# A hand-ordered attention and mixture kernel: the order of all engines and the PSUM banks from row 2 on, drawn anew

## The chip, the cores and the metric

The kernel runs on one core of a Trainium2 chip. The metric is the device time of one execution in microseconds (us). The core has five engines that run side by side, each with its own instruction queue that is worked off in order: TensorE (PE, matrix products; its weight loads are shown as PEld), VectorE (DVE), ScalarE (ACT), GpSimd (POOL) and SyncE (SP, which here only issues transfers). Sixteen DMA engines move data between device memory (HBM) and the on-chip memory (SBUF). Matrix products land in PSUM, which has eight banks. Engines wait for each other by semaphores.

## The reference

Eight batch rows, eight heads, 576 tokens, head size 64. Half of the heads see the last 32 tokens, the other half every fourth of the last 128:

```python
    scores = scale * np.matmul(q, k.transpose(0, 1, 3, 2))
    mask_plain = (rel >= 0) & (rel < window)
    mask_dil = (rel >= 0) & (rel < window * dilation) & (rel % dilation == 0)
    scores = np.where(masks[None, :, :, :], scores, -1000000000.0)
    attn = np.exp(scores - max); attn = attn / sum
    x = np.matmul(attn, v)
```

What the heads of a token give, side by side, is a vector x of 512. A gate picks two of eight experts, and each adds a product of rank 16:

```python
    logits = x @ w_gate
    topk = the two largest; w = softmax of their logits
    out = x + sum over the two experts of w * ((x @ A[e]) @ B[e])
```

## The kernel before

The kernel is a list of small steps and a text, PLAN, that says in which order they are issued. The engine of a step is fixed, and so each engine gets the steps of the text that are its own, in the text's order. "S041@4" means that step S041 takes PSUM banks from number 4 on. A step waits for the steps that make its inputs, for those that last read a buffer that it overwrites, and, where it is the first user of its banks, for all users that these banks had before. The waits are worked out from the text when the program is built. So a new text changes two things: what stands ahead of a step in its engine's queue, and whose banks it has to wait for.

A step's name has a letter, sometimes a part, then the batch row r (0 to 7) and the group of heads g (0 plain, 1 dilated). S041 is the first part of the scores of row 4, group 1. For one row the work runs like this:

| step | engine | line | what it does |
|---|---|---|---|
| L, Lk, Lq, Lv | POOL issues | 272, 275 | loads of the row's q, k and v into one of four buffers, changed to bf16 on the way; L4 to L6 are two transfers each; row 7 comes in eight pieces (Lq7gh, Lv7gh) |
| S0rg, S1rg | PE | 212 | scores of five and of four blocks: 24 and 20 matmuls, two banks |
| E0rg, E1rg | ACT | 345 | exponential of these scores |
| Vrg | PE | 212 | 26 matmuls with v, three banks |
| Rrg, Nrg | DVE | 381, 384 | reciprocal of the sums, and the division |
| Brg | POOL | 391 | cast to bf16 (half of B71 is Bx7, on ACT) |
| Trg, Ur | PE | 408, 432 | transposes, 8 and 2 matmuls |
| Crg, Cdr, Cpr | ACT | 418 to 442 | copies of these to SBUF (Cx7 on DVE) |
| Z0r, Z1r | PE | 212 | products with A and the gate, 12 and 8 matmuls |
| Y0r, Y1r | ACT | 466 | copies to SBUF |
| m0, m1, s12, tt, top, g2 | DVE | 478 to 488 | gate values: the two largest logits, and their weights; th (ACT, 485) is a step in the middle of it |
| gzr | POOL | 493 | weights times the products (row 7: DVE) |
| Gr | PE | 498 | transposes, 5 matmuls (row 7: G7, H7) |
| gnr, gcr | ACT | 517, 514 | copies of these |
| Dr0, Dr1, Dr2 | PE | 212 | products with B, 4 matmuls each |
| Ar0, Ar1, Ar2 | DVE | 545, 575 | added to x; for late rows parts go by way of ACT (dx 571, dy 551) to POOL (A42 to A72 573; A53, A63, A73 553) |
| Or | SP | 586, 590 | store of the row; two halves for rows 6 and 7 |

F0 to F3 and "warm" are matmuls on zeros whose results nobody reads; pz, vz and xz set parts of buffers to zero, and cc and cd build the mask constants.

Line 212 is the helper that issues nearly all matmuls, so most TensorE rows of the profile carry it, and the names of the tiles tell them apart: "ps<-one" and "ps<-con,one" open a score step (24 or 20 matmuls, of which the first four write the mask), "ps<-in" are the rest of it, "ps<-in,p" is V, "ps<-aw,xt" is Z, "ps<-bt,gn" and "ps<-bt,gc" are D.

Rows overlap: while row r's scores are made, the adapters (T to A) of the rows before it are still on their way. A load of row r may start when row r-4 has used its buffer for the last time. All transfers of a queue run in the order in which they are issued. The stores wait for the last pieces of row 7's load (all Lq, and Lv710 and Lv711), and store number n also for the landing of store number n-2:

```python
            if name[0] == "O":
                if len(name) == 2:
                    o.deps = o.deps + stores[-2:-1]
                stores.append(name)
```

The order that the banks set is made here:

```python
            if o.bank is not None and o.bank.users[0] == name:
                o.bank.at = int(at)
                for b in range(o.bank.at, o.bank.at + o.bank.size):
                    o.deps = o.deps + held[b]
                    held[b] = list(o.bank.users)
```

Of the kernel before, what the change touches and what calls it, by code (L numbers as in the profile page):

```python
# [593 lines left out]


PLAN = """
pz0 wz warm@4 F1@1 awf btf vz00 pz2 con vz10 Lk00 Lk01 Lv00 Lv01
S000@6 vz01 vz11 tab cc1 cd3 vz20 cc0 vz21 cd2 cd0 L11 pz1 E000
F2@1 L10 cd1 S100@4 S101@6 E100 E101 L2 S001@2 E001 V00@4 R00 N00 V01@1
L3 R01 F0@0 xz0 B00 N01 B01 T00@4 vz30 L4 pz3 C00 S111@5 E111  # L600
awc S011@2 U0@0 T01@7 E011 V11@3 Cd0 Cp0 S010@1 C01 R11 vz31 E010 N11
Z00@0 Y00 m00 Z10@6 Y10 m10 S110@4 B11 s120 E110 tt0 th0 top0 V10@2
g20 gz0 T11@5 R10 N10 btc G0@1 gc0 D01@6 B10 gn0 D00@0 C11 xz1
U1@4 Cd1 Cp1 T10@5 C10 A01 A00 S121@6 E121 S120@3 S021@1 Z01@0 E021 Z11@5
Y01 m01 Y11 m11 L5 s121 S020@1 D02@0 V21@5 E120 top1 tt1 th1 g21
E020 A02 V20@0 R21 N21 R20 gz1 G1@5 gn1 F3@6 S130@6 N20 gc1 B21 E130
S031@3 D12@2 E031 S030@0 D10@5 T21@7 E030 C21 A12 S131@3 B20 V30@0 A10 E131
U2@7 T20@6 R30 N30 Cp2 B30 L6 V31@3 Cd2 C20 Z02@7 Y02 Z12@1 R31
N31 B31 T30@2 D11@6 Y12 C30 S041@4 A11 E041 S141@2 S140@6 m02 E141 S040@0
m12 s122 tt2 U3@5 Cp3 th2 E040 top2 Cd3 g22 gz2 V41@2 T31@0 E140  # L610
C31 V40@5 R41 N41 Z03@2 G2@0 Y03 gn2 Z13@1 gc2 R40 Y13 N40 B40
S051@2 D20@4 E051 A20 m13 S151@6 E151 Lq700 S050@0 S150@2 E150 m03 s123 V51@5
top3 tt3 T40@3 th3 Lq701 E050 C40 B41 g23 T41@4 C41 R51 Lq710 V50@0
N51 R50 D22@5 N50 U4@7 gz3 Cd4 Cp4 G3@6 gn3 D21@3 gc3 A22 A21
Z04@7 Y04 B50 Lq711 S060@0 D32@2 Z14@7 S161@5 m04 E060 Y14 m14 E161 s124
S160@0 A32 Lv710 T50@7 E160 D30@3 S061@5 top4 V60@0 A30 tt4 R60 C50 Lv711
O1 E061 B51 T51@3 N60 C51 V61@4 th4 g24 R61 N61 U5@7 S171@2 Cp5
Cd5 S070@0 Z05@7 E171 E070 Z15@6 Y05 S170@2 S071@4 Y15 Lv700 m05 m15 top5
Lv701 B60 gz4 E170 E071 s125 G4@0 B61 D31@6 tt5 th5 gn4 V70@1 T60@4
A31 gc4 V71@5 U6@0 C60 O0 g25 O2 gz5 G5@4 Cp6 Cd6 R70 N70  # L620
B70 T61@2 D41@0 D42@3 R71 N71 gn5 A41 C61 dx4 gc5 B71 Bx7 D40@5
Z06@2 Y06 Z16@4 Y16 A40 m06 A42 D52@3 m16 s126 dx5 top6 U7@7 Cp7
Cd7 tt6 T71@1 Cx7 C71 T70@4 D51@5 A52 th6 g26 A51 D50@0 A50 C70
gz6 Z07@2 Z17 m07 m17 s127 tt7 dy5 G6@5 gc6 O3 D61@0 th7 gn6
D62@7 A53 top7 O4 dx6 g27 D60@5 gy7 gz7 A62 dy6 O5 A61 A63
O61 G7@3 H7 gm7 gn7 gc7 D72@0 dx7 A72 D71@1 A60 D73@6 O60 A71
D70@7 O71 A70 dy7 A73 O70
"""

_INS = ["qkv", "aw", "bt", "con"]  # L630
# [60 lines left out]
```

## Time and profile before

| | |
|---|---|
| median of 3 runs | 101.25 us (100.71 to 101.56) |
| the profiled execution | 101.17 us, its span 99.4 us |
| busy share of the span: PE, ACT, DVE, POOL | 82%, 71%, 62%, 52% |
| mean granted TensorE clock | 0.977 |
| HBM read and written | 29.07 MB and 9.44 MB, 387 GB/s over the span |
| row 3's scores start | 39.73 us |
| row 4's scores start | 48.43 us |
| row 5's, row 6's, row 7's | 56.81, 65.94, 73.27 us |
| last value matmuls (V71) end | 80.24 us |
| stores issued | from 72.37 to 95.22 us |

The span runs from the first to the last instruction; the time of an execution is somewhat longer, and the profiled one has both. Times inside the profile are microseconds from the start of the span. "Issue" in the chain of waits is time in which an engine waited for nothing that the profile shows. Matmuls overlap, so their price in the queue is read from one start to the next. The trace names instructions by line and tile; the step names used here follow from the order of PLAN, since each engine works its queue off in order.

### The profile page before, as it was taken

The numbers are of one execution on the slowest core, as the hardware profiler recorded it, in microseconds if no ns is written. First come the engines' busy times: TensorE is split into PE (matmuls) and PEld (weight loads), VectorE is DVE, ScalarE is ACT, GpSimd is POOL, SyncE is SP. The second block draws the span as 40 slices with busy tenths as digits, with TensorE's granted clock in tenths as the row PEclk, the third lists the DMA queues.
The fourth block names the chain that finished last, engine by engine and source line by source line (L and its number), as shares of the span: only waits on it lengthen the run. The fifth ranks groups of instructions, "written<-read, shape, count | busy, mean of one in ns | idle before, by whom it ended". The sixth has DMA issues, their size and how long they took to land.

```text
span 99.4 us, 3604 instructions
## 1 busy us (share of the span) xinstructions
PE 81.2 (82%) x1587; PEld 59.8 (60%) x1587; DVE 62.0 (62%) x138; ACT 71.0 (71%) x123; POOL 51.6 (52%) x68
## 2 busy tenths in 40 slices
PE   3999969869568988999995968999999999777500
PEld 2443557458445864889674847877888878564300
DVE  5770008606469188259736665796895999979810
ACT  5294592499858964796895695979989989957400
POOL 5999402851548054404922095449458365574820
PEclk9999999999999999999999999999999999999955
DMA  1999999999999999999999999997999999839994
GB/s 19 318 206 207 207 216 228 209 209 214 207 211 217 218 216 208 209 214 205 216 208 214 218 210 210 219 197 122 198 326 408 415 412 412 352 163 415 386 421 202
DMA packets 5727, 24.50 MB, mean 247 GB/s; under 512 B 720, under 2 KB 848, under 8 KB 4944
## 3 DMA queue, kind: packets, MB, share of 16 engines
q0 software_dynamic: 3840, 14.23, 72.5%
q1 hardware_dynamic: 1728, 9.77, 24.1%
q8 instruction: 12, 0.20, 0.8%
q10 hardware_dynamic: 144, 0.28, 0.7%
q14 instruction: 3, 0.02, 0.1%
HBM read 29.07 MB, written 9.44 MB: 387 GB/s over the span
## 4 chain that ended last, share of the span: by engine, by line
PE 43%; DMA 28%; DVE 9%; ACT 6%; POOL 4%; issue 4%; POOLq 0%
PE ps L212 39%; DMA in<-in_qkv_dram 28%; DVE x L384 4%; PE ps L408 3%; ACT p L345 2%; DVE x L545 2%; POOL xb L391 2%; POOL x L553 1%; PE ps L498 1%; ACT gn L517 1%; ACT xt L418 1%; DVE rec L381 1%; POOL x L573 1%; DVE top L486 1%; ACT gc L514 1%
## 5 line engine op out<-in xcount | busy, mean ns | idle before, releaser
L391 POOL CAST xb<-x 128x1152 bf16<-128x1152 f32 (+1 forms) x16 | 18.2, 1140 | 27.6 <-DVE x L384 27.6
L345 ACT ACTIVATE p<-ps 128x960 bf16<-128x960 f32 (+1 forms) x32 | 27.6, 899 | 5.5 <-PE ps L212 5.4
L212 PE MATMUL ps<-in,p 128*64 128x130 bf16 (+1 forms) x416 | 21.3, 221 | 3.3 <-ACT p L345 3.1
L384 DVE TENSOR_TENSOR x<-ps,rec 128x1152 f32<-128x1152 f32 x16 | 21.7, 1357 | 0.5
L212 PEld LDWEIGHTS ps<-in,p 128*64 128x64 bf16 (+1 forms) x416 | 17.1, 104 | 6.7 <-ACT p L345 4.4
L545 DVE TENSOR_TENSOR x<-x,ps 128x1024 f32<-128x1024 f32 (+1 forms) x16 | 17.5, 1115 | 3.4 <-PE ps L212 3.4
L381 DVE RECIPROCAL rec<-ps 128x18 f32<-128x18 f32 x16 | 4.3, 270 | 17.4 <-PE ps L212 17.2
L493 POOL TENSOR_TENSOR gz<-zs,g 128x640 bf16<-128x640 f32 x7 | 8.9, 1275 | 11.1 <-DVE g L488 11.1
L212 PE MATMUL ps<-warm 128*128 128x512 f32 x22 | 12.7, 720 | 1.5 <-DVE warm L216 1.5
L212 PE MATMUL ps<-in 64*64 64x96 bf16 (+1 forms) x576 | 11.9, 201 | 1.5 <-issue 1.5
L212 PEld LDWEIGHTS ps<-in 64*64 64x64 bf16 x576 | 10.9, 106 | 3.7 <-issue 1.8
L272 POOL DMA_DIRECT2D in<-in_qkv_dram x22 | 11.7, 587 | 0.8 <-POOLq L674 0.8
L212 PE MATMUL ps<-aw,xt 128*128 128x136 bf16 x160 | 11.3, 223 | 0.1
L408 PE MATMUL ps<-one,xb 128*128 128x128 bf16 x128 | 9.6, 219 | 1.2 <-issue 1.2
L418 ACT COPY xt<-ps 128x1024 bf16<-128x1024 bf16 x8 | 8.1, 1011 | 3.4 <-PE ps L408 3.3
L212 PEld LDWEIGHTS ps<-aw,xt 128*128 128x128 bf16 x160 | 9.6, 98 | 0.9 <-ACT xt L418 0.4
L408 PEld LDWEIGHTS ps<-one,xb 128*128 128x128 bf16 x128 | 7.6, 97 | 2.5 <-issue 1.3
L212 PEld LDWEIGHTS ps<-warm 128*128 128x128 f32 x22 | 4.7, 232 | 6.3 <-issue 4.8
L421 ACT COPY xt<-ps 128x1024 bf16<-128x1024 bf16 x7 | 7.2, 1034 | 1.4 <-PE ps L408 1.4
L212 PE MATMUL ps<-bt,gn 128*128 128x256 bf16 (+1 forms) x48 | 6.8, 263 | 1.5 <-ACT gn L517 0.8
L212 PE MATMUL ps<-bt,gc 128*128 128x256 bf16 (+1 forms) x48 | 6.6, 255 | 1.5 <-ACT gc L514 1.5
L466 ACT COPY zs<-ps 128x408 f32<-128x408 f32 (+1 forms) x14 | 5.9, 459 | 2.0 <-PE ps L212 2.0
(54 smaller groups left out, 98.0 us busy)
## 6 DMA issues: line engine op xcount, KB each, us to landing
in<-in_qkv_dram POOLq DMA_DIRECT2D x10, 868.5 KB, 23.1
out_dram<-x SPq DMA_DIRECT2D x6, 1152.0 KB, 5.8
in<-in_qkv_dram POOLq DMA_DIRECT2D x10, 288.0 KB, 8.1
out_dram<-x SPq DMA_DIRECT2D x4, 576.0 KB, 3.0
in<-in_qkv_dram POOLq DMA_DIRECT2D x10, 146.2 KB, 8.1
in<-in_qkv_dram POOLq DMA_DIRECT2D x2, 434.2 KB, 13.5
awf<-in_aw_dram ACTq DMA_DIRECT2D x1, 272.0 KB, 3.7
btf<-in_bt_dram SPq DMA_DIRECT2D x1, 256.0 KB, 3.5
```

What stands on the lines that cost most here:

```text
L212: return nc.tensor.matmul(o, lhsT=lhsT, rhs=rhs, start=start, stop=stop, skip_group_check=True)
L272: nc.gpsimd.dma_start(out=IN[r % SLOTS][half(a), at : at + n], in_=qkv[r, a, :, at - 2 * VB * a : at - 2 * VB * a + n],) if n < ROW else n ...
L345: return [nc.scalar.activation(p[:, :, :].rearrange("p h (s c) -> p h s c", c=PER)[:, :, b0 : b0 + nb, 0:SEG], PS[:, k.at : k.at + 2, 0 : ...
L381: rc = add(f"R{tag}", "DVE", ("el", 60), lambda: [nc.vector.reciprocal(rec[:, :].rearrange("p (b i) -> p b i", b=3), PS[:, k.at : k.at + 3 ...
L384: nm = add(f"N{tag}", "DVE", ("el", XG), lambda: [nc.vector.tensor_tensor(X[r][:, XG * g : XG * g + XG].rearrange("p (b i n) -> p b i n", ...
L391: add(f"B{tag}", "POOL", ("el", cut), lambda: [nc.gpsimd.tensor_copy(XB[r % 2][:, g, 0:cut], X[r][:, XG * g : XG * g + cut])], [nm] + free)
L408: nc.tensor.transpose(tp[j][:, 128 * u : 128 * u + 128], xb[:, g, 256 * u + 128 * j : 256 * u + 128 * j + 128], ident())
L418: return [nc.scalar.copy(xt[:, 0:2, 0:S].rearrange("p j (c i) -> p j c i", c=C)[:, :, :, 0:128], tp.rearrange("p j (i c) -> p j c i", c=C))]
L421: return [nc.scalar.copy(xt[:, 2:4, 0:512], tp)]
L466: zc.append(add(f"Y{st}{r}", "ACT", ("el", len(us) * ZW), lambda us=us, k=k: [nc.scalar.copy(zs[:, us[0] : us[-1] + 1].rearrange("p u n -> ...
L493: return [en.tensor_tensor(GZ[i][:, us[0] : us[0] + n, :].rearrange("p u (e r) -> p u e r", e=E), zv()[:, us[0] : us[0] + n, 0:ER].rearran ...
L545: return [nc.vector.tensor_tensor(v, v, PS[:, k.at : k.at + nk].rearrange("p b n -> p (b n)"), ALU.add)]
```

## The change

PLAN is the same up to U1's copies and S121. From there all words are the same, but their order and the bank numbers differ, for all engines. No step is added or removed, and no step's code changes.

```diff
-S121@6 E121 S120@3 S021@1 Z01@0 E021 Z11@5
-Y01 m01 Y11 m11 L5 s121 S020@1 D02@0 V21@5 E120 top1 tt1 th1 g21
-E020 A02 V20@0 R21 N21 R20 gz1 G1@5 gn1 F3@6 S130@6 N20 gc1 B21 E130
-S031@3 D12@2 E031 S030@0 D10@5 T21@7 E030 C21 A12 S131@3 B20 V30@0 A10 E131
-U2@7 T20@6 R30 N30 Cp2 B30 L6 V31@3 Cd2 C20 Z02@7 Y02 Z12@1 R31
-N31 B31 T30@2 D11@6 Y12 C30 S041@4 A11 E041 S141@2 S140@6 m02 E141 S040@0
-m12 s122 tt2 U3@5 Cp3 th2 E040 top2 Cd3 g22 gz2 V41@2 T31@0 E140
-C31 V40@5 R41 N41 Z03@2 G2@0 Y03 gn2 Z13@1 gc2 R40 Y13 N40 B40
-S051@2 D20@4 E051 A20 m13 S151@6 E151 Lq700 S050@0 S150@2 E150 m03 s123 V51@5
-top3 tt3 T40@3 th3 Lq701 E050 C40 B41 g23 T41@4 C41 R51 Lq710 V50@0
-N51 R50 D22@5 N50 U4@7 gz3 Cd4 Cp4 G3@6 gn3 D21@3 gc3 A22 A21
-Z04@7 Y04 B50 Lq711 S060@0 D32@2 Z14@7 S161@5 m04 E060 Y14 m14 E161 s124
-S160@0 A32 Lv710 T50@7 E160 D30@3 S061@5 top4 V60@0 A30 tt4 R60 C50 Lv711
-O1 E061 B51 T51@3 N60 C51 V61@4 th4 g24 R61 N61 U5@7 S171@2 Cp5
-Cd5 S070@0 Z05@7 E171 E070 Z15@6 Y05 S170@2 S071@4 Y15 Lv700 m05 m15 top5
-Lv701 B60 gz4 E170 E071 s125 G4@0 B61 D31@6 tt5 th5 gn4 V70@1 T60@4
-A31 gc4 V71@5 U6@0 C60 O0 g25 O2 gz5 G5@4 Cp6 Cd6 R70 N70
-B70 T61@2 D41@0 D42@3 R71 N71 gn5 A41 C61 dx4 gc5 B71 Bx7 D40@5
-Z06@2 Y06 Z16@4 Y16 A40 m06 A42 D52@3 m16 s126 dx5 top6 U7@7 Cp7
-Cd7 tt6 T71@1 Cx7 C71 T70@4 D51@5 A52 th6 g26 A51 D50@0 A50 C70
-gz6 Z07@2 Z17 m07 m17 s127 tt7 dy5 G6@5 gc6 O3 D61@0 th7 gn6
+S121@6 E121 S021@3 D02@2 E021 Z11@5 Z01@0 Y01 A02 Y11 m11 S020@1 E020
+S120@3 L5 E120 V21@5 F3@0 m01 top1 s121 tt1 th1 g21 gz1 R21 V20@0 N21
+B21 G1@5 R20 N20 S030@3 gc1 gn1 S130@6 E030 S031@1 E130 S131@3 D10@5 A10
+E031 T21@7 C21 V30@0 R30 B20 N30 E131 L6 U2@7 Cp2 T20@6 Cd2 V31@3 C20
+R31 Z12@6 N31 Z02@0 Y12 Y02 m02 S140@6 E140 m12 B30 top2 S041@1 S141@3
+D11@6 T30@5 s122 tt2 E041 S040@0 th2 g22 gz2 E141 A11 V41@2 R41 N41 G2@7
+E040 B31 C30 T31@1 gn2 D20@5 C31 V40@2 U3@0 B41 gc2 T41@7 A20 Cd3 S151@5
+Cp3 D12@1 C41 E151 R40 Z03@0 Y03 N40 B40 Z13@4 A12 Y13 S051@6 m03 D22@5
+U4@0 m13 s123 E051 S150@3 A22 tt3 th3 top3 S050@1 g23 V51@5 Cd4 E150 R51
+gz3 N51 E050 Cp4 T40@4 V50@1 C40 G3@0 Lq710 Z14@5 R50 gn3 N50 Z04@4
+D21@6 gc3 Y14 Y04 Lq701 A21 S060@0 m04 E060 S161@4 D30@2 D32@7 m14
+S160@0 E161 s124 A30 B51 T51@6 S061@4 E160 C51 E061 A32 V60@0 tt4 th4
+Lq711 Lq700 Lv710 R60 B50 T50@3 C50 V61@4 N60 R61 Lv711 U5@7 Cd5 Cp5
+S171@2 E171 N61 S070@0 Z05@7 top4 g24 E070 O0 Y05 m05 Z15@6 Y15 m15 s125
+S170@2 E170 S071@4 O2 E071 top5 tt5 D31@6 Lv700 A31 Lv701 gz4 G4@0 th5
+g25 V70@1 R70 N70 gn4 B60 gc4 T60@4 V71@5 B61 C60 U6@0 gz5 G5@2 Cd6 Cp6
+R71 gn5 N71 T61@3 C61 D41@0 B70 D42@4 dx4 gc5 A42 Bx7 D40@6 Z06@5 B71
+A41 Z16@2 Y06 Y16 A40 m06 D52@3 dx5 m16 top6 U7@0 T71@4 O3 s126 Cd7 Cp7
+T70@7 C71 tt6 th6 Cx7 g26 D50@0 D51@5 C70 Z07@2 Z17 A50 A52 A51 dy5 O1
...
```

Taken apart by engine, in the stretches that differ most: on TensorE, T30, D11 and D12 now follow row 4's first score step (S140) rather than lead it, and Z03 and Z13 follow row 5's first score step (S151). On GpSimd, gz2 stands before B31, gz4 before B60 and B61, A42 before B71, L6 before B30, and row 7's load pieces stand in the order Lq710, Lq701, Lq711, Lq700, Lv710, Lv711, Lv700, Lv701 (before: Lq700, Lq701, Lq710, Lq711, Lv710, Lv711, Lv700, Lv701). SyncE stores O0, O2, O3, O1, O4 and so on (before: O1, O0, O2, O3, O4).

More of the change, by code (lines that the diff above doesn't have):

```diff
@@ L596 @@
 PLAN = """
[L597 to L604, printed above, removed]
@@ L621 @@
-B70 T61@2 D41@0 D42@3 R71 N71 gn5 A41 C61 dx4 gc5 B71 Bx7 D40@5
-Z06@2 Y06 Z16@4 Y16 A40 m06 A42 D52@3 m16 s126 dx5 top6 U7@7 Cp7
-Cd7 tt6 T71@1 Cx7 C71 T70@4 D51@5 A52 th6 g26 A51 D50@0 A50 C70
-gz6 Z07@2 Z17 m07 m17 s127 tt7 dy5 G6@5 gc6 O3 D61@0 th7 gn6
-D62@7 A53 top7 O4 dx6 g27 D60@5 gy7 gz7 A62 dy6 O5 A61 A63
-O61 G7@3 H7 gm7 gn7 gc7 D72@0 dx7 A72 D71@1 A60 D73@6 O60 A71
-D70@7 O71 A70 dy7 A73 O70
+pz0 wz warm@4 F1@1 awf btf vz00 pz2 con vz10 Lk00 Lk01 Lv00 Lv01 S000@6
+vz01 vz11 tab cc1 cd3 vz20 cc0 vz21 cd2 cd0 L11 pz1 E000 F2@1 L10 cd1
@@ new lines @@
+S100@4 S101@6 E100 E101 L2 S001@2 E001 V00@4 R00 N00 V01@1 L3 R01 F0@0
+xz0 B00 N01 B01 T00@4 vz30 L4 pz3 C00 S111@5 E111 awc S011@2 U0@0 T01@7
+E011 V11@3 Cd0 Cp0 S010@1 C01 R11 vz31 E010 N11 Z00@0 Y00 m00 Z10@6 Y10
+m10 S110@4 B11 s120 E110 tt0 th0 top0 V10@2 g20 gz0 T11@5 R10 N10 btc
+G0@1 gc0 D01@6 B10 gn0 D00@0 C11 xz1 U1@4 Cd1 Cp1 T10@5 C10 A01 A00
+S121@6 E121 S021@3 D02@2 E021 Z11@5 Z01@0 Y01 A02 Y11 m11 S020@1 E020
+S120@3 L5 E120 V21@5 F3@0 m01 top1 s121 tt1 th1 g21 gz1 R21 V20@0 N21
@@ L628 @@
+A41 Z16@2 Y06 Y16 A40 m06 D52@3 dx5 m16 top6 U7@0 T71@4 O3 s126 Cd7 Cp7
+T70@7 C71 tt6 th6 Cx7 g26 D50@0 D51@5 C70 Z07@2 Z17 A50 A52 A51 dy5 O1
+O4 gz6 m07 m17 s127 tt7 G6@7 top7 gc6 th7 g27 gy7 gz7 A53 gn6 D61@0
+D62@5 dx6 A62 D60@6 A61 dy6 G7@4 H7 gm7 gn7 A63 gc7 O5 A60 O61 O60 D72@1
+D71@2 D73@5 dx7 A72 A71 dy7 O71 D70@5 A70 A73 O70
 """
```

## The prediction

> **What bounds the kernel now.** I read the page's head and slices first, then the chain that ended last, then the windows between the stalls that the chain shows, then the timeline of single engines.
>
> ```profile
> span 99.4 us, 3604 instructions
> DMA  1999999999999999999999999997999999839994
> q8 instruction: 12, 0.20, 0.8%
> ...
> 20.58 27.80 DMA in<-in_qkv_dram
> 48.43 0.72 PE ps L212 x24
> 52.43 1.18 issue
> 58.82 1.30 issue
> 66.39 0.24 issue
> ```
>
> In the row of tenths the DMA engines are full nearly from start to end, first with loads, then with stores. The chain says which side is late when. Up to 48.38 it is a transfer: the second half of L4, issued at 20.58 and landed 27.80 later. After that the chain runs along TensorE alone up to the last value matmuls of row 7 (V71), apart from one pair of exponentials at 49.16 and three holes called "issue", in which TensorE waits for no semaphore. From V71 on it is the latency of row 7's adapter.
>
> ```profile
> 48.40:53.60 5.20, 3.77 (x118) 2.75 (x119) 3.50 (x12) 4.33 (x8) 2.47 (x3) 1.00 1.06 209
> 53.60:60.10 6.50, 5.21 (x127) 4.19 (x126) 4.02 (x11) 4.46 (x7) 2.97 (x4) 1.00 1.06 213
> 60.10:66.60 6.50, 6.27 (x126) 5.31 (x127) 4.82 (x9) 5.53 (x10) 2.84 (x4) 1.00 1.05 213
> ```
>
> These are windows that end where the holes end (length, then busy time and count for PE, PEld, DVE, ACT, POOL, then clock, DMA share, GB/s). Between holes lie 127 and 126 matmuls with as many weight loads, so 254 instructions and a few waits. Queue q8 moved 0.20 MB in 12 packets, about 16 KB each. I read the holes as TensorE waiting for its next block of some 256 instructions, which has to come through the same full DMA engines: a block costs 6.5 us here, whatever the matmuls in it need. The blocks are counted in instructions, so the block boundaries stay at the same place in the count when the order changes.
>
> [...]
>
> **The change part by part.** No instruction is added, so all durations are those of before; what changes is what stands ahead of what. I follow the new order from the point that both orders share.
>
> ```profile
> 42.97 1.33 PE L212 MATMUL ps<-in,p 128*64 128x130 bf16 x26
> 44.14 0.27 PE L432 MATMUL ps<-one,xb 128*128 128x128 bf16 x2
> 45.97 1.35 PE L212 MATMUL ps<-aw,xt 128*128 128x136 bf16 x20
> 47.27 0.62 PE L408 MATMUL ps<-one,xb 128*128 128x128 bf16 x8
> 47.73 0.60 PE L212 MATMUL ps<-bt,gc 128*128 128x256 bf16 x4
> 48.43 0.40 PE L212 MATMUL ps<-con,one 64*64 64x480 bf16 x4
> 48.99 0.36 PE L212 MATMUL ps<-con,one 64*64 64x384 bf16 x4
> ```
>
> Prices on TensorE are taken from start to start, since matmuls overlap: V 1.17 (42.97 to 44.14), a pair Z 1.30 (45.97 to 47.27; I split it 0.72 and 0.58), T 0.46 (47.27 to 47.73), a five-block S 0.56 (48.43 to 48.99), a four-block S 0.4. A full D is priced like T; the small D2 at 0.23.
>
> *Rows 2 and 3, up to 48.4.* L4 is issued before the first difference, so it lands at 48.38 in both. The new order runs S021, D02 and S020 earlier and S120 later, and puts the row 3 scores together (S030, S130, S031, S131). They start when L3 has landed, at 39.7 as before. ScalarE then has E030, E130, E031, C21 and E131 in a row, so V31 starts near 44.95 (before 44.79). T20's copy C20 is done near 46.4, then Z12 and Z02 last until 47.75. The next step, S140, needs L4. So everything that moved here is covered by the wait for L4, with 0.6 us to spare. But T30, D11 and D12 (8, 4 and 4 matmuls), which before filled TensorE until L4 came, now stand behind it: 0.46 + 0.46 + 0.23 = **1.15 us more TensorE work after 48.4**, and the same amount idle ahead of it.
>
> *From 48.4 to row 6's scores (S060).* In instructions, the first row 4 matmul stands 16 matmuls earlier in the count. Before, the boundary of the block lay 9 matmuls ahead of S041 (127 less the 118 of the first window), inside T30, about 47.45. Now it lies 7 matmuls into S140, at 48.55: 1.1 us later. From there three blocks took 53.61 - 47.45 = 6.16, then 6.5 and 6.5 us. Counting through the new order, the boundaries fall on the third matmul of T31, the eighth of S150 and the first of S060.
>
> What the work alone would allow, by the waits of the new order:
>
> ```profile
> L345 ACT ACTIVATE p<-ps 128x960 bf16<-128x960 f32 x16 | 15.5, 975 | 2.9 <-PE ps L212 2.9
> L345 ACT ACTIVATE p<-ps 128x768 bf16<-128x768 f32 x16 | 13.0, 823 | 2.5 <-PE ps L212 2.5
> L384 DVE TENSOR_TENSOR x<-ps,rec 128x1152 f32<-128x1152 f32 x16 | 21.7, 1357 | 0.5
> L391 POOL CAST xb<-x 128x1152 bf16<-128x1152 f32 x15 | 17.6, 1175 | 27.0 <-DVE x L384 27.0
> L493 POOL TENSOR_TENSOR gz<-zs,g 128x640 bf16<-128x640 f32 x7 | 8.9, 1275 | 11.1 <-DVE g L488 11.1
> L418 ACT COPY xt<-ps 128x1024 bf16<-128x1024 bf16 x8 | 8.1, 1011 | 3.4 <-PE ps L408 3.3
> ```
>
> E140, E041, th2 and E141 follow one another on ScalarE from 48.95, to 51.8; V41 waits for E141, ends at 53.0. On GpSimd gz2 now stands ahead of B31. It waits for th2 and g22 (51.2), ends at 52.5, and B31 at 53.65. T31 is queued behind it on TensorE, and D20, V40, U3, T41 and S151 behind T31. So T31 starts at 53.65 by its data and at 48.55 + 6.16 = 54.7 by its block; the block decides, and the move of gz2 costs nothing while 1.05 us of slack last. Then V40 55.5, S151 57.3 (L5 is there: second half issued at 31.22, landed 25.6 later, 56.8), D12, Z03, Z13, S051 59.3, S150 60.2 (Z13's copy frees its bank). Its block is there at 54.7 + 6.5 = 61.2: 0.9 us lost. Then S050, V51, T40, V50 (63.65), G3, Z14, Z04, D21, and S060 would start at 66.85. L6 is there (65.1: issued at 47.83, 17.3 to landing), but the third block would be there only at 61.2 + 6.5 = 67.7. Without any fetch wait the same walk gives 66.05. Before, S060 started at 65.94.
>
> ```profile
> 30.54 1.30 POOL L275 DMA_DIRECT2D in<-in_qkv_dram  x2
> DMA to landing us min/median/max: 22.1/23.8/25.6
> ...
> 47.16 1.30 POOL L275 DMA_DIRECT2D in<-in_qkv_dram  x2
> DMA to landing us min/median/max: 13.8/15.5/17.3
> ...
> 65.94 0.40 PE L212 MATMUL ps<-one 64*64 64x480 bf16 x4
> 72.98 0.27 PE L432 MATMUL ps<-one,xb 128*128 128x128 bf16 x2
> 78.90 1.34 PE L212 MATMUL ps<-in,p 128*64 128x130 bf16 x26
> ```
>
> So S060's bounds are 66.05 and 67.7. I take 67.3, the middle between 66.85 and 67.7: the third block is asked for as L6 ends, and what follows are smaller transfers.
>
> *From S060 to the end of V71.* Before: U5 at 72.98 and V71's end at 80.24, that is 7.04 and 7.26 more. The new order has Z14 (0.58) already behind it and not the hole of 0.24, which leaves 6.22 to U5. But ScalarE runs E060, E161, E160, C51, E061 without a pause from 0.65 after S060's start: 0.95 + 0.8 + 0.8 + 1.0 + 0.95 = 4.5, so V61 starts at 5.15 and U5 at 6.35. The bank move of D30 to the banks that V60 needs adds a wait for A30, which ends 0.15 before E160 does, hence free. From U5 on the order is that of before but for gz4 (a rival below). Sum 6.35 + 7.26 = 13.6: V71 ends at 80.9, **0.65 later than before**.
>
> *Behind V71* only neighbours change places: A42 before B71, D50 and A50 before D51 and A51, top6 before s126, Cd before Cp. Bx7 on ScalarE is the later half of what T71 waits for, so B71 has about 0.2 of cover. D40's new bank spares it 0.25 (it waited for N71), which Z06 gives back, as its copies end no sooner. I cost all this at nothing; uncovered, A42 ahead of B71 would cost up to 0.73, less that 0.2.
>
> *Transfers.* L6 is issued some 5 us earlier, past B30, and still lands behind L5. Row 7's pieces go in another order: Lq711, Lq700 and Lv710 leave behind B51 near 65.7 (before Lq711 left at 66.95), Lv711 behind B50 near 68.5 (before 68.02). The pieces issued on a short queue took 4.0 to 4.3 us to land, so the last that the stores wait for lands at 72.5 to 72.8 (before 68.02 + 4.3 = 72.3).
>
> ```profile
> 66.95 1.62 POOL L272 DMA_DIRECT2D in<-in_qkv_dram  x3
> DMA to landing us min/median/max: 4.1/4.2/4.3
> ...
> 93.89 1.26 POOL x L553
> DMA to landing us min/median/max: 3.0/3.2/3.4
> ```
>
> The stores' new order (O0, O2, O3, O1) changes no last one. The last store leaves when A73 (93.89 + 1.26) is done, and needs 3.4 us; both move with V71.
>
> **Sum.** S060 starts at 67.3 in place of 65.94 (+1.36), V71 ends 13.6 behind it in place of 14.3 (-0.7): +0.65, and nothing behind it. Span 100.05. The profiled execution took 101.17 around its span of 99.4 and lies 0.08 below the median of 101.25. So 101.17 + 0.65 = **101.8**, 0.5% above the median.
>
> **Rivals.** *Slower, by the GpSimd queue.* gz4 now stands ahead of B60, and g24 behind N61. From V61's end: R61, N61, top4, g24 put gz4 at 8.45 after S060; gz4, B60, B61, gz5 are then 1.28 + 1.15 + 1.14 + 1.28 = 4.85, ending at 13.3. G5 wants gz5 just behind V71, at 13.6. From 0.3 us of delay on, every further step of this queue goes into G5, B70 and the whole tail. For it: single casts and maxima stretch next to GpSimd work (the 40 gate values of top cost 445 ns in the mean, one B took 1.54 where 1.175 is the mean). With the full 6.5 us in the third block (+0.4) and 0.6 of such delay: 102.8.
>
> ```profile
> L486 DVE TENSOR_TENSOR top<-zs,mx 128x40 f32<-128x40 f32 x7 | 3.1, 445 | 0.0
> 18.46 1.54 POOL L391 CAST xb<-x 128x1152 bf16<-128x1152 f32 x1 [0.43 <-DVE x L384]
> ```
>
> *Faster: instruction blocks come in time.* Then S060 starts at 66.05, V71 ends at 79.65, 0.6 earlier: 100.5, and by as much less as the walk's waits are too long. Against it: three blocks in a row were late. For it: the third was late by 0.24 only, and the new order has waits of its own in which a block can come.
>
> *The order does not matter*, because landings at 48.4, 56.8 and 65.1 pace both: 101.2. Against it: before reached S060 0.8 after its landing, so it was not paced by it.
>
> **How the numbers follow.** Forecast 0.40, slow queue 0.33, blocks in time 0.20, no effect 0.07. About 1% (1.0 us) is what a measurement of this kernel can tell from no change. Faster by more (under 100.2) takes the lower part of the second rival: 0.14. Slower by more takes the first rival and the upper edge of the forecast (S060 at 67.7 gives 102.2): 0.39. Within 1%: 0.47. The range leaves out a tenth at each end: 100.1 to 103.1.
>
> **What would show it.** Right: TensorE idle for about 0.6 us ahead of 48.4, and then holes called "issue" inside T31 and S150, 127 matmuls apart; S060 near 67.3; V71's end near 80.9 and the tail 19.1 behind it. Wrong: no holes between 48 and 67 (second rival), or G5, T60 or T71 waiting for GpSimd (first), or a new wait in rows 2 and 3 that makes S140 start well after 48.4.

## The result and the profile after

The changed kernel takes **104.31 us** in the median (103.0 to 105.34, six executions), the kernel before 101.58 beside it: a ratio of 1.026, 95% interval 1.020 to 1.032. The forecast was 101.8, and the time lies above its range. Some executions on this chip are disturbed and longer whatever the kernel; ratios leave those out, and where too few others were left for a ratio, the times of the undisturbed ones are given alone.

The profiled execution took 103.0 us, the shortest of the six, with a span of 101.2. So the profiles account for 1.8 us, and the medians differ by 2.7 (the rest stays open, as the part on the prediction says). First the head and slices of the page after:

```profile
span 101.2 us, 3601 instructions
...
DMA  2999999999999999999999999999989499939995
GB/s 19 306 211 204 214 217 206 217 213 212 209 226 209 209 218 218 209 219 212 211 215 216 219 205 196 149 208 184 179 354 404 189 408 408 422 164 390 390 417 206
```

The transfers look as before, with one difference: the place of a dip. After, the rate falls to 149 GB/s in slice 26 of 40, from 63.3 to 65.8 us; before, such a dip (122) lies in slice 28, from 67.1 to 69.6 us:

```profile
GB/s 19 318 206 207 207 216 228 209 209 214 207 211 217 218 216 208 209 214 205 216 208 214 218 210 210 219 197 122 198 326 408 415 412 412 352 163 415 386 421 202
```

Then the chain of after that ended last (start, length, what):

```profile
19.88 28.24 DMA in<-in_qkv_dram
48.16 0.62 PE ps L212 x20
...
53.73 0.42 issue
...
68.64 1.74 PE ps L212 x49
70.39 1.21 issue
71.59 0.22 PE ps L212
...
77.12 1.02 DVE top L486
78.15 1.08 DVE tt L483
79.23 1.13 DVE x L545
```

Up to 48.16 it is still L4. One hole, of 0.42, is left where the forecast saw two of about 1 us. Two things are new: a hole of 1.21 at 70.39, and VectorE on the chain ahead of V71, with top5 and tt5 at over 1 us each. The windows from S060's start to V71's start, of before and then of after (length, busy time and count of PE, PEld, DVE, ACT, POOL, then clock, DMA share, GB/s), show that this is the whole loss:

```profile
65.94:78.90 12.96, 12.71 (x328) 10.39 (x327) 10.05 (x29) 11.67 (x21) 8.40 (x11) 1.00 0.98 280
```

```profile
65.66:80.51 14.85, 12.41 (x319) 10.08 (x318) 10.95 (x27) 11.35 (x20) 6.91 (x9) 1.00 0.93 262
```

S060 starts 0.28 earlier, the stretch is 1.89 longer, and from V71's start to the end of the span it is 20.69 against 20.50. That is -0.28 + 1.89 + 0.19 = 1.80, the difference of the spans. TensorE idles 2.44 us in the stretch (14.85 less 12.41) where it idled 0.25, at two places in its timeline:

```profile
69.11 1.27 PE L212 MATMUL ps<-in,p 128*64 128x130 bf16 x25
71.59 0.22 PE L212 MATMUL ps<-in,p 128*128 128x130 bf16 x1 [1.21 <-issue]
...
80.51 1.34 PE L212 MATMUL ps<-in,p 128*64 128x130 bf16 x26 [1.18 <-DVE g L488]
```

**The hole** stands ahead of the last matmul of V60, about 127 matmuls behind the block boundary at S060: the next block came late. Before, the same boundary had no hole. **The wait** is V71's. Its three banks start at 5, and bank 6 held D31, which A31 reads; A31 ended at 80.37 (the profile names the gate step just behind it on VectorE). Why A31 is late is seen on VectorE and GpSimd, after:

```profile
77.04 1.11 DVE L486 TENSOR_TENSOR top<-zs,mx 128x40 f32<-128x40 f32 x1
78.07 1.16 DVE L483 SCALAR_TENSOR_TENSOR tt<-zs,s 128x40 f32<-128x40 f32 x1
79.16 1.21 DVE L545 TENSOR_TENSOR x<-x,ps 128x1024 f32<-128x1024 f32 x1
```

```profile
75.73 1.27 POOL L493 TENSOR_TENSOR gz<-zs,g 128x640 bf16<-128x640 f32 x1 [6.61 <-DVE g L488]
76.95 2.23 POOL L391 CAST xb<-x 128x1152 bf16<-128x1152 f32 x2
```

and before:

```profile
76.57 0.20 DVE L486 TENSOR_TENSOR top<-zs,mx 128x40 f32<-128x40 f32 x1
...
76.88 0.20 DVE L483 SCALAR_TENSOR_TENSOR tt<-zs,s 128x40 f32<-128x40 f32 x1
```

```profile
73.19 1.15 POOL L391 CAST xb<-x 128x1152 bf16<-128x1152 f32 x1 [2.52 <-DVE x L384]
74.30 1.28 POOL L493 TENSOR_TENSOR gz<-zs,g 128x640 bf16<-128x640 f32 x1
75.53 1.14 POOL L391 CAST xb<-x 128x1152 bf16<-128x1152 f32 x1
```

Before, GpSimd was done with B61 at 76.67, 0.1 us after top5 began, and top5 took its 0.20. After, gz4 stands ahead of both casts, which run from 76.95 to 79.18; top5 ends at 78.15 with the first, tt5 at 79.23 with the second. Both read two tiles from SBUF. The steps beside them that read one take no longer than elsewhere: the maxima 0.30 for three, the one-input sum 0.17 (before, with GpSimd idle, 0.30 at 34.44 and 0.17 at 35.00). Nor does a sum with one input from PSUM; A31 itself starts only as the second cast ends, but in the kernel before such a sum takes 1.21 at 66.04, beside a cast that runs from 65.86 to 67.01, and 1.22 at 77.29 with GpSimd idle.

### The profile page after: what moved, and what is told of

Its sections match the earlier page's. It is cut to its first block, busy times and chain, and to the rows that moved or that the text cites. A ratio compares the mean times of both kernels' runs of the same rounds, so it can differ in the third digit from the quotient of the medians.

```text
span 101.2 us, 3601 instructions
## 1 busy us (share of the span) xinstructions
PE 81.5 (80%) x1587; PEld 59.5 (59%) x1587; DVE 62.8 (62%) x138; ACT 71.4 (71%) x123; POOL 51.5 (51%) x68
## 3 DMA queue, kind: packets, MB, share of 16 engines
q0 software_dynamic: 3840, 14.23, 71.1%
## 4 chain that ended last, share of the span: by engine, by line
PE 36%; DMA 28%; ACT 11%; DVE 11%; POOL 6%; issue 3%; POOLq 0%
PE ps L212 31%; DMA in<-in_qkv_dram 28%; ACT p L345 4%; DVE x L384 4%; PE ps L408 3%; POOL xb L391 3%; PE ps L498 2%; DVE tt L483 2%; ACT gn L517 2%; POOL gz L493 1%; POOL x L553 1%; DVE top L486 1%; ACT gc L514 1%; DVE x L545 1%; ACT xt L421 1%
## 5 line engine op out<-in xcount | busy, mean ns | idle before, releaser
L212 PEld LDWEIGHTS ps<-in,p 128*64 128x64 bf16 (+1 forms) x416 | 17.1, 104 | 7.8 <-ACT p L345 3.1
L545 DVE TENSOR_TENSOR x<-x,ps 128x1024 f32<-128x1024 f32 (+1 forms) x16 | 17.7, 1116 | 4.9 <-PE ps L212 4.8
L212 PE MATMUL ps<-warm 128*128 128x512 f32 x22 | 12.0, 684 | 1.5 <-DVE warm L216 1.5
L514 ACT COPY gc<-ps 128x576 bf16<-128x576 bf16 x7 | 4.5, 645 | 5.3 <-PE ps L498 5.3
(54 smaller groups left out, 99.5 us busy)
## 6 DMA issues: line engine op xcount, KB each, us to landing
in<-in_qkv_dram POOLq DMA_DIRECT2D x2, 434.2 KB, 13.6
```

What stands on the lines that cost most here:

```text
L212: return nc.tensor.matmul(o, lhsT=lhsT, rhs=rhs, start=start, stop=stop, skip_group_check=True)
L514: gc = add(f"gc{r}", "ACT", ("el", S), lambda k=k: [nc.scalar.copy(GC[i][:, :], bank(k).bitcast(BF)[:, 0:S])], gt + dfree, k)
L545: return [nc.vector.tensor_tensor(v, v, PS[:, k.at : k.at + nk].rearrange("p b n -> p (b n)"), ALU.add)]
```

## The experiments

All kernels below do the same work; only the place of the named steps differs. Three causes were on the table: the **collision** of top5 and tt5 with the casts; the **late block** in V60, either because a block takes a fixed time or because it queues behind loads; and row 7's **loads**, of which the last that a store needs landed at 73.0 (72.3 before; SP issued the first store at 73.08 and 72.37). Where the chain runs, by profile (start of the first matmul, us):

| kernel | S060 | V60 | V61 | V71 | span |
|---|---|---|---|---|---|
| before | 65.94 | 70.09 | 71.80 | 78.90 | 99.4 |
| after | 65.66 | 69.11 | 72.19 | 80.51 | 101.2 |
| a0 again | 65.54 | 69.03 | 72.65 | 80.97 | 101.7 |
| a1 g24 early | 67.11 | 70.55 | 74.18 | 81.26 | 101.8 |
| b1 gz4 late | 65.32 | 69.11 | 70.95 | 78.97 | 99.5 |
| b2 loads early | 65.33 | 69.75 | 72.69 | 79.79 | 100.2 |
| a2 loads later | 66.26 | 69.75 | 71.50 | 79.83 | 101.6 |
| h1 new, then old | 65.48 | 69.36 | 72.14 | 79.23 | 100.9 |
| h2 old, then new | 65.80 | 69.20 | 71.84 | 80.17 | 100.9 |
| c1 repaired | 65.42 | 69.14 | 72.48 | 79.56 | 100.1 |
| c4 loads only | 66.59 | 70.59 | 73.38 | 81.70 | 102.4 |
| c5 dry spell | 65.27 | 69.27 | 71.02 | 78.62 | 99.4 |

**The changed kernel once more** (a0, no edit).

> The changed kernel once more, for a second trace. Theory (two VectorE steps, top5 and tt5, wait out the GpSimd casts B60 and B61; an instruction hole inside V60; G5's new bank): top5 and tt5 take about 1.1 us each again in place of 0.2, V71 waits about 1.2 us for A31, and 103 to 104.5 us. Rival (the first trace shows accidents of one execution): the stretched steps are not there and the loss sits elsewhere.

103.29 us, ratio 1.021 (1.012 to 1.030). The same three things: top5 1.11, tt5 1.16, V71 waiting 1.18, a hole of 1.74 in V60. So neither is an accident of one profile; the hole's length varies.

**The collision, taken out of after** (a1).

```diff
-tt4 th4 Lq711 Lq700 Lv710 ... Z05@7 top4 g24 E070
+tt4 th4 top4 g24 Lq711 Lq700 Lv710 ... Z05@7 E070
```

> The changed kernel with two VectorE steps (top4, g24) moved ahead of R60, nothing else. Theory: gz4 then runs near 71 in place of 75.7, B60 near 73.6 and B61 near 75.3, so that both casts are over when top5 and tt5 come at 77: these take 0.2 us each, A31 starts near 77.5 in place of 79.2, V71 no longer waits for it (-1.2 us) and the time falls by 1.2 to 1.6 us. Rival (the loss comes from the instruction hole in V60, or from the bank of G5): below 0.4 us.

With g24 earlier, gz4 runs long before B60, and top5 and tt5 take 0.19 and 0.20:

```profile
79.03 0.19 DVE L486 TENSOR_TENSOR top<-zs,mx 128x40 f32<-128x40 f32 x1
79.15 0.20 DVE L483 SCALAR_TENSOR_TENSOR tt<-zs,s 128x40 f32<-128x40 f32 x1
```

V61 to V71 falls from 8.32 to 7.08 (before 7.10): the collision accounts for all of that stretch. But the time did not fall by the 1.2 to 1.6 us that were expected: 104.07, ratio 1.029 (1.017 to 1.041). In its profile L4 landed 0.7 later, the holes were longer (0.85 in T31, 1.76 in V60), and S060 came at 67.11. The gain is there in its stretch and does not reach the end.

**The collision, put into before** (b1).

```diff
-th4 g24 R61 N61 U5@7 ... Lv701 B60 gz4 E170
+th4 R61 N61 g24 U5@7 ... Lv701 gz4 B60 E170
```

> The kernel before with this one part of the change: g24 behind N61 on VectorE, and B60 behind gz4 on GpSimd. Theory: gz4 at 75.1, B60 to 77.5, B61 to 78.7; top5 and tt5 meet them and end with them, A31 at 78.7 in place of 77.3, V71 near 79.9 in place of 78.9: +1.0 to +1.3 us on the kernel before. Rival (order of GpSimd has 2 us of slack here, since G5 and T60 come later): within 0.3 us.

The collision appears: top5 0.90 and tt5 0.97, and V71 waits 0.85 for A31, V61 to V71 8.02 in place of 7.10. VectorE and GpSimd in this kernel:

```profile
75.71 0.90 DVE L486 TENSOR_TENSOR top<-zs,mx 128x40 f32<-128x40 f32 x1
76.52 0.15 DVE L480 TENSOR_REDUCE s<-mx 128x5 f32<-128x10 f32 x1
76.71 0.97 DVE L483 SCALAR_TENSOR_TENSOR tt<-zs,s 128x40 f32<-128x40 f32 x1
```

```profile
75.41 2.22 POOL L391 CAST xb<-x 128x1152 bf16<-128x1152 f32 x2
```

Together with a1 this shows the collision in both directions. The sixteen profiles of this document agree: 34 times a top or tt with two SBUF inputs starts while a GpSimd cast or sum still has 0.16 us or more to run, and each time it ends 0.05 to 0.07 us behind that step; of the 177 that start while none runs, one takes more than 0.20 (0.33). Two of the four executions of b1 took 101.26 and 101.27 (the others 103.02 and 103.31), with 100.7 as the median of the kernel before beside them. S060 came 0.6 earlier in this profile, so the end does not give the price.

**Loads sooner in before** (b2).

```diff
-Lq710 V50@0 ... B50 Lq711 ... Lv710 ... Lv711
+Lq710 Lq711 Lv710 Lv711 V50@0 ... B50 ...
```

> The kernel before with Lq711, Lv710 and Lv711 issued right behind Lq710, ahead of gz3 and B50, so that the queue of loads no longer runs dry near 68.7 us. Theory (a block of instructions for TensorE waits behind the queued loads; before, the dry spell let the block for matmul 1236 through early): a hole of 0.8 to 1.5 us called issue appears near 71 us inside V61, where the kernel before has none, V71 ends about 1 us later, although the loads land 1 us sooner. Rival (earlier loads help or do nothing): no hole, time the same or up to 1 us less.

102.12, ratio 1.009 (1.003 to 1.015): a little longer. The loads landed no sooner (the last needed one at 72.6), and V60 now has a hole of 1.05, V60 to V61 2.94 in place of 1.71. Filling the load queue made the hole in the order of before.

**Loads later in after** (a2), and with the collision out as well (a3, the edit of a1 added).

```diff
-th4 Lq711 Lq700 Lv710 R60 B50 T50@3
+th4 R60 B50 Lq711 Lq700 Lv710 T50@3
```

> The changed kernel with Lq711, Lq700 and Lv710 issued behind B50 in place of ahead of it (GpSimd order alone). Theory (the block of instructions for matmul 1236 is late because the queue of loads never runs dry): the loads land about 1 us later, but the hole of 1.2 to 1.7 us inside V60 shrinks below 0.6, V61 starts about 1 us sooner after S060. The stretch of top5 and tt5 stays, the time falls by 0.5 to 1.2 us. Rival (the hole belongs to the place in the count): hole as before, time the same or worse by the later loads.

The hole is gone (V60 to V61 1.75), the collision stays (1.15, 1.16), as it should. 104.3, ratio 1.030 (1.020 to 1.041): not the expected gain, since the first store now leaves at 75.65, and the stores before it are still at work when the last one comes. The last four stores, issue to landing, after and then a2:

```profile
DMA to landing us min/median/max: 2.8/2.9/3.2
```

```profile
DMA to landing us min/median/max: 3.9/4.0/4.3
```

V71 starts 0.68 earlier than after, and 1.1 us is given back behind it.

> The changed kernel with both repairs: top4 and g24 ahead of R60, and the three loads behind B50. Theory (the loss behind S060 is the hole in V60 and A31 held back by top5 and tt5): from S060's start to V71's start 12.8 to 13.3 us as in the kernel before (12.96), in place of 14.85 and 15.43; time within 0.7 us of the kernel before. Rival (another part of the new order costs the time): 14 us or more, time over 1.5 us above the kernel before.

Its profile is of an execution of 104.03 us, so only its order of events counts: no hole in V60, no collision, stores from 75.52 with the transfers busy almost to the end. The last store leaves when A73 is done (96.54) and takes 4.9 us to land, where it took 3.2 in after. The shortest of the four executions took 101.85 (before: 101.4), the others 104.03 to 104.45. With both stalls out, the late stores are the likely limit; this profile does not settle it.

**Halves of the order**: new up to S060, then the rest in the order of before (h1), and the reverse (h2).

```diff
 h1 (on the new order)
-Lq701 A21 S060@0 m04 E060 S161@4 D30@2
+Lq701 A21 Lq700 B50 Lq711 S060@0 D32@2 S161@5 m04 E060
 h2 (on the old order)
-Y04 B50 Lq711 S060@0 D32@2 Z14@7 S161@5
+Y04 B50 Lq711 Z14@5 Y14 S060@0 m04 E060 S161@4 D30@2 D32@7
```

> The new order up to S060, and from there on what is left in the order and with the banks of the kernel before. Theory (the loss lies wholly behind S060): S060 near 65.6, no hole in V60, no stretched top5 and tt5, time of the kernel before or up to 0.5 us less. Rival (the new order of rows 2 to 5 costs 0.5 us or more, as the prediction had it): S060 at 66.5 or later and 0.5 to 1 us more than the kernel before.

> The order of the kernel before up to S060, and from there on what is left in the new order and with its banks. Here Lq711 still leaves behind B50, so by theory the hole in V60 is absent or below 0.6, while gz4, B60 and B61 meet top5 and tt5 (about 0.9 to 1.1 us each) and V71 waits about 1.2 us for A31: 1.0 to 1.6 us more than the kernel before. Rival (the loss comes from the stretch up to S060): within 0.5 us of the kernel before.

h1: 102.64 and 102.13 (two more took 103.77 and 104.08), against a median of 101.4 for the kernel before beside them; a hole of 0.84, no collision (top5, tt5 0.20), first store at 74.17. h2: 102.55, ratio 1.012 (1.003 to 1.022); a hole of 0.76, collision as in after (1.11, 1.16, V71 waiting 1.18). Each half costs about 1%. The collision belongs to the second half alone. The hole was expected with neither and comes with either, which speaks for the state of the load queue and against one place in the new text.

**Collision and late loads, both repaired in after** (c1, and once more as c1_repeat).

```diff
-U3@0 B41 gc2 ... N40 B40 Z13@4 ... G3@0 Lq710 Z14@5 ... Y04 Lq701 A21
+U3@0 B41 Lq710 Lq701 gc2 ... N40 B40 Lq700 Z13@4 ... G3@0 Z14@5 ... Y04 A21
-tt4 th4 Lq711 Lq700 Lv710 R60 ... Z05@7 top4 g24 E070
+tt4 th4 top4 g24 Lq711 Lv710 R60 ... Z05@7 E070
```

> The changed kernel with top4 and g24 ahead of R60, and with Lq710 and Lq701 issued behind B41 and Lq700 behind B40, ahead of gz3 (Lq711 and the rest stay behind B51 and B50). Theory: the queue of loads no longer runs dry near 63 us, the loads land by 72.5 and the stores start near 72.4 as in the kernel before; the dry spell comes near 67 to 69 again, so the hole in V60 is below 0.6; top5 and tt5 take 0.2 each. S060 at 65.6, V71's start at 78.4 to 79.0, time 0.3 to 1 us below the kernel before. Rival (loads or stores set the end whatever the order): same as the kernel before or slower.

> The repaired kernel again on the same chip as the run beside it, for the comparison: hole of 0.9 to 1.5 us in V60, 101.8 to 102.5 us, 1.0% to 1.5% above the kernel before.

102.14, ratio 1.013 (1.007 to 1.019), and 102.12, 1.011 (1.005 to 1.017). The first store leaves at 72.34 and 72.23, top5 and tt5 take 0.20. What is left is the hole, 1.47 both times. It was expected to shrink below 0.6, and the time to come out below the kernel before: both missed, as the loads still filled the queue from 67 to 69 us (shown below).

**Only the loads of c1** (c4: c1 without the move of top4 and g24).

> The changed kernel with the three loads earlier alone (as in the first run of this call), top4 and g24 left where they are. Theory: the stores start about 0.7 us sooner and the hole in V60 shrinks to under 0.6, but top5 and tt5 (1.1 us each) still hold A31 and with it V71 by about 1.2 us: 0.7 to 1.5 us above the first run of this call, and 0.5 to 1.5 us below the changed kernel.

103.95, ratio 1.030 (1.021 to 1.038), collision as in after. Against c1, on the same chip, the medians differ by 103.95 - 102.14 = 1.8 us. In the profiles 8.32 - 7.08 = 1.24 lies between V61 and V71, which is the collision's price there. S060 is 1.2 later in c4, by no doing of the edit: row 4's load landed 0.66 later (48.48, in c1 47.82), and the hole in T31 was 0.71 in place of 0.16. The hole in V60 was 0.92, not under 0.6 as expected. So the loads alone gain nothing, and the collision alone (a1) gained nothing; with both repaired the ratio falls from 1.026 and 1.021 (after, a0) to 1.013 and 1.011.

**Another collision, taken out**: top6 takes 0.76 in the kernel before, on the chain, while A52 runs on GpSimd; in the new order it is tt6, with 0.54. A52 goes behind gz6, in c1 (c2, edit below) and in before (c3, the same move).

```diff
-Z17 A50 A52 A51 dy5 O1 O4 gz6 m07
+Z17 A50 A51 dy5 O1 O4 gz6 A52 m07
```

> The kernel of the run before this one, with A52 behind gz6 on GpSimd, so that tt6 meets no running GpSimd step. Theory: tt6 takes 0.2 in place of 0.54, th6 and C70 come 0.2 to 0.3 sooner, and since A53 ends up to 0.3 later, the net is 0 to 0.3 us less. Rival: O5 waits for A53, and the stores behind it move the end by +0.2 to +0.4.

> The kernel before with A52 behind gz6 alone. Theory: top6 takes 0.2 in place of 0.75 on the chain that ends last; th6 and C70 follow ScalarE's own order, so Z07 comes 0.15 to 0.4 sooner and the time falls by 0.1 to 0.4 us. Rival: A53 and O5 are late by as much, no gain or +0.3.

top6 takes 0.19 in c3, but the time stays: 101.67, ratio 1.002 (0.997 to 1.007). In c2 tt6 takes 0.20, and the time is 103.37, 1.023 (1.018 to 1.029), with A53 only at 89.92 behind A52 on GpSimd. So the step that was moved out of VectorE's way holds up what stands behind it on its own engine. That is the smaller part of c2's loss: from V71's start to the end of the span it is 0.3 longer than c1 (20.9 and 20.5), and the rest lies ahead of V71, where the edit changes nothing (S060 at 66.97, in c1 65.42).

**A dry spell in the load queue** (c5: c1 with two loads behind B50, so that they leave at 66.28 and 66.85, not at 64.71 and 65.28; TensorE's order is that of c1).

```diff
-top4 g24 Lq711 Lv710 R60 B50 T50@3
+top4 g24 R60 B50 Lq711 Lv710 T50@3
```

> The repaired kernel (top4 and g24 early, Lq710, Lq701 and Lq700 early) with Lq711 and Lv710 moved behind B50, so that they leave near 66.9 as in the kernel before and the queue runs dry when TensorE asks for the block of matmul 1236. Theory: the hole of 1.47 us inside V60 falls below 0.3, the loads still land by 72.5 to 73, and the time falls by 0.8 to 1.4 us against the repaired kernel: level with the kernel before or up to 0.5 below. Rival (the stores, which start as late as the last loads land, take it back, as in the two runs with all three loads behind B50): hole gone, but the last store lands no sooner, gain below 0.4.

The hole is gone: V60 to V61 1.75, in c1 3.34. V60 and what follows, in c1 and then in c5:

```profile
69.14 1.27 PE L212 MATMUL ps<-in,p 128*64 128x130 bf16 x25
71.89 0.22 PE L212 MATMUL ps<-in,p 128*128 128x130 bf16 x1 [1.47 <-issue]
```

```profile
69.27 1.33 PE L212 MATMUL ps<-in,p 128*64 128x130 bf16 x26
```

Two of the six executions took 101.2 and 100.95, level with the kernel before (median 101.1 beside them); the other four took 102.57 to 103.14. So that all three repairs together bring the time back is likely, but two executions are too few to show it. Queue q8 brings instructions (0.20 MB over the span), q0 loads (14.23 MB); here is what each moved from 67 to 69 us and, where q8 has nothing there, from 69 to 71 (packets, MB, share of 16 engines). Before, then c5:

```profile
q0 software_dynamic: 56, 0.20, 74.9%
q8 instruction: 1, 0.02, 2.8%
```

```profile
q0 software_dynamic: 76, 0.29, 92.8%
q8 instruction: 1, 0.02, 2.8%
```

In after, 67 to 69 and then 69 to 71:

```profile
q0 software_dynamic: 109, 0.38, 103.9%
```

```profile
q0 software_dynamic: 143, 0.38, 101.0%
q8 instruction: 1, 0.02, 2.8%
```

and the same two stretches in c1:

```profile
q0 software_dynamic: 124, 0.41, 103.6%
```

```profile
q0 software_dynamic: 200, 0.38, 104.3%
q8 instruction: 1, 0.02, 3.0%
```

Where the loads leave the engines some time, the block comes in that stretch and V60 has no hole; where they fill them, it comes one stretch later and V60 has one of 1.21 and 1.47. a2 (q0 at 55.8% there) is of the first kind, b2 (106.8%, hole 1.05) of the second. Since c1 and c5 have the same order on TensorE and differ only in when these loads leave, this shows the load queue as the cause of this hole.

## Why the prediction was wrong

*Up to 48.4: right.* S140 at 48.16 (48.4 forecast), paced by L4. The idle time ahead of it was smaller, though: TensorE worked until 48.1, where I had 0.6 of slack.

*From there to S060: right by the walk, wrong by the blocks.* The walk without fetch waits gave 66.05; measured 65.66, and 65.54 in a0. T31 was to start at 53.65 by its data and did so at 53.34; S151 at 57.3 with the block's wait in it, measured 56.81. The prediction does not show how 66.05 follows step by step, so part of the closeness may be luck. **The first step that failed is "a block costs 6.5 us here"**: behind the hole in T31, 127 matmuls ran in 5.84 us, with TensorE busy throughout:

```profile
54.16:60.00 5.84, 5.84 (x127) 4.65 (x126) 4.31 (x12) 4.88 (x9) 2.30 (x2) 1.00 1.06 215
```

The hole in T31 was 0.42 of the 1.05 that I had, that in S150 (0.9) did not come, and so S060's forecast delay of 1.36 did not either. A fixed time per block was a fit through three holes. What the runs show is a delay until the packet gets through, which depends on how full the load queue is (q0 at 92.8% of the engines from 67 to 69 us and no hole in c5, 103.6% and a hole of 1.47 in c1). "Blocks in time" (0.20) was no better: V60's block was late in ten of the fifteen profiles of altered orders.

*From S060 to V71's end, 13.6: wrong by 2.6.* It took 81.85 - 65.66 = 16.19: U5 came 7.71 behind S060 (6.35 forecast), and V71's end 8.48 behind U5 (7.26 forecast). This is where the time went, by two steps, one in each term:

- **No hole was charged behind S060.** The next boundary had none before, and so I gave it none. I named no cover for that. The cover was the load queue's dry spell, the dip of before (the DMA engines at 0.80 from 66 to 68 us and 0.90 from 68 to 70). The change moved it to about 62 to 66 (0.93 and 0.88 in these two stretches of 2 us, and then 1.07 and 1.02), too early for V60's block, and V60 lost 1.21. I had only asked where the loads land, not where their queue is empty.
- **The collision was not in the sum.** V71 lost 1.18 by it. The row "top 445 ns" stood in the prediction, as a sign that steps "stretch next to GpSimd work". Its mean hid the collision. By line, before has (min/median/max):

```profile
L486 DVE TENSOR_TENSOR top<-zs,mx x7: 190/200/856, 26.1 to 84.8; 128x40 f32<-128x40 f32 x7
```

Four of some 0.20, and top3, top4 and top6 at 0.86, 0.73 and 0.76, each ending just behind a GpSimd step: top3 at 60.55 behind B41 (60.48). The change moved gz4 ahead of B60 and put the casts where top5 stands; the prediction priced only what is queued behind them on GpSimd. In the trace of after the steps with two SBUF inputs took 1.11 and 1.16 in place of 0.20, ending 0.06 and 0.05 us behind the casts, and those with one SBUF input did not stretch (0.17 for the sum beside the first cast). What makes a step end with the cast beside it, no run shows.

*The slow GpSimd queue* (0.33) named the right step, gz4 ahead of B60, and the right sign. Its path was wrong: it went by gz5 and G5, and the delay ran by top5, tt5, A31 and V71's banks. G5 did wait, until 82.19, but for its new bank, which N70 held until 82.05; I had that at nothing.

*Behind V71: nearly right*: +0.19 where I had nothing. *Transfers*: I had the last needed load at 72.5 to 72.8; it landed at 73.0. Lq710 left only at 62.15 behind gz3, and the queue ran short behind L6, which is the likely reason. That cost nothing in after, where the last store still waited for A73 (issued at 97.26), but it leaves no room: a2 shows the price of 2.6 us more.

*The sum.* In the profiles S060 came 1.64 earlier than forecast, the stretch to V71's end was 2.59 longer, and the tail 0.2: the span missed by 1.15 only, because the two large errors have opposite signs. That is luck. The profiled execution, at 103.0, lies within the forecast's range; the median of the six is 1.3 above that execution.

*Open:* from row 4's first scores to S060 the new order takes 17.7 on average (ten profiles, without a3's; 17.1 to 18.5), the old one 17.0 (five, 16.4 to 17.5). The pair compared here has 17.50 and 17.51. In the new order this stretch grows with the holes in it: 17.10 with none (c1_repeat), 17.50 with 0.42 (after), 18.45 with 1.27 (c2). So T31's hole did come in most of them, of up to 1.09. This, and the hole in V60 (1.21 in after, 1.74 in a0), may be the part of the medians that the pair of profiles does not account for; no run took it apart.

## What to carry to other kernels

When an order is changed, ask of each engine not only who waits for whom, but what runs at the same moment: a short two-input step on VectorE can take as long as the GpSimd cast beside it (here 1.11 and 1.16 us in place of 0.20, beside two casts of 2.23 together), and a row whose maximum is four times its median says so (here 0.856 to 0.200). A stall that is absent is also held off by something; find what, as the gap in the load queue of the kernel before (q0 at 74.9% from 67 to 69 us), before charging nothing for it. And one repair at a time can show no gain: here no single repair of the collision, the hole or the late loads moved the end, and two together did (c1).

## What the runs showed of the hardware

Two short VectorE steps of 0.20 us with two SBUF inputs grew to 1.11 and 1.16 beside GpSimd casts, while steps with one input from SBUF (0.17) or with one of two from PSUM (1.21, with GpSimd idle 1.22) did not. With one and the same TensorE order, an instruction block's packet started at 68.0 or at 69.5 us (c5 and c1, packet records of the trace), according to whether the load queue left the DMA engines idle (q0 at 92.8% of them from 67 to 69 us in c5, 103.6% in c1); from the packet's start to the matmul behind the hole it took 2.2 us more (after: 69.35 to 71.59), and 2.2 to 3.0 over all the holes of the sixteen profiles. And the load queue ran short before its last load had landed: in after two loads left at 62.15 and 62.73, 2.4 and 1.9 us before L6 landed (64.58), and still the rate fell to 149 GB/s in one slice, with 196 and 208 beside it.
